# Linear attention into an eight-expert MoE: x^T stored in the order of the output rows, and output tiles that leave in one transfer

## The chip, the cores and the metric

The kernel runs on one core of a Trainium2 chip. The metric is device time in microseconds, from the start to the end of one execution. Engines are called as the profile calls them: PE is TensorE, PEld its weight loads, DVE VectorE, ACT ScalarE, POOL GpSimd, SP SyncE (which here only issues transfers). SBUF is the on-chip memory with 128 partitions, PSUM the accumulation memory of PE.

## What is computed

Inputs are q, k and v of shape (8, 8, 576, 64) (batch, head, position, channel), a gate matrix (512, 8) and two weight stacks w1 (8, 512, 1024) and w2 (8, 1024, 512). The output has 4608 rows of 512 fp32 numbers, one row for each token (8 batches of 576 positions).

```python
phi(x) = where(x > 0, x, exp(x) - 1) + 1
kv  = einsum('bhsd,bhse->bhde', phi(k), v);  z = sum(phi(k), axis=2)
num = phi(q) @ kv;  den = phi(q) . z + 1e-6
x   = (num / den), heads side by side: 4608 rows (batch, position), 512 columns
P   = exp(x @ w_gate - max)
8 times: P /= row sums; P /= column sums; P *= 4608 / 8
out = sum over e of P[:, e] * (relu(x @ w1[e]) @ w2[e])
```

## The kernel before

**Two stages that overlap.** The first is an attention front. For each batch and each group of four heads (16 units in all) `att` loads k, q and v, forms phi of k and q, and accumulates kv and z on PE (`f_kv`, L427). It transposes phi(q) on PE (L453), copies it as `qpT` (L345 or L343), multiplies it by z for the denominator and by kv for the numerator (`heads`, L482 to L486, called by `f_den` and `f_num`), and takes 1/den as exp(-ln(den)) on ACT (L497, L502). In the end `f_x` (L511 to L513) multiplies the numerator in PSUM by 1/den and writes x^T to SBUF as fp16. `xT` has the 512 channels on partitions (four blocks of 128) and all 4608 tokens along the free axis. A unit is done in two halves (c = 0, 1) of 288 tokens (CH = 288), so `f_x` runs 32 times, each over two blocks of channels, 576 elements per partition.

**The order of tokens in x^T.** k, q and v are loaded with 64 partitions for one head, partition w holding positions 9w to 9w + 8 (NJ = 9, PW = 64). Transposed, the columns stand as (j, w): all positions 9w + 0 first, then all 9w + 1, and so on. A half is a contiguous run of 288 of these columns, and x^T keeps that order, so column j * 64 + w of a batch is position 9w + j.

**The second stage** is the MoE. For expert 0 most groups of 512 tokens use plain products (L701 first layer, L996 second layer); from then on both layers use a seven-product scheme on 2 x 2 blocks, with sums and differences of blocks formed by DVE (`x_blocks` L746 to L751, `combos` L1038 and L1052, `f_S` L1083), matmuls at L816 and L1112, and DVE (L1143) or ACT with POOL (L1150, L1153) adding P times the product to the fp32 accumulators `acc`. x^T and its block differences are stored to DRAM (`xd`), and later experts load them by transfers from SP's queue (`x_load`, L793). The routing P (`logits` L529, `sinkhorn` L551 to L587) is made per token in the order of x^T; it runs on DVE and PE behind the front. Among its steps are L563, which writes its product transposed, and L586, which writes its product packed.

**Output.** Expert 7 ends the sums. `out_dma` (L967 to L974) sends a tile of 128 tokens in two transfers of 64 partitions each. The 64 tokens of a half have the same j, so their rows lie nine rows apart in the output. The transfers go by SP's queue; in the last two groups of tokens the second half goes by ACT's.

**The end.** The last group of the last expert uses plain products again (`last`, L1189 to L1222): tiles 3, 2 and 1 in whole (512 columns), tile 0 in two pieces of 256 columns, each piece with eight matmuls (L1208), a DVE step that scales and adds (L1217), and its transfers. `pl = (p_hq, p_att)[i % 2]` gives the pieces two kinds of PSUM buffers by turns.

**What sets the order.** `_Plan` is a list scheduler that runs while the kernel is built: each task has engines with a cost, what it depends on, a priority, and groups of buffers that it takes (`acq`) or uses. A buffer pool of size n lets a task take a buffer only when all users of the n-th group before are done. Numerator and `f_kv` share the pool `p_kv` of size 1. For the front, `_FRONT` (L141 to L218) writes the order of tasks out by number and engine, so that order does not depend on costs. In the later part a chain of dependencies (L1281 to L1293) fixes the order of PE's tasks, and priorities and costs decide the rest. Each engine and each queue takes its instructions in the order in which they were issued.

Of the kernel before, what the change touches and what calls it, by code (L numbers as in the profile page):

```python
# [13 lines left out]
ALU = mybir.AluOpType  # L14
# [3 lines left out]
class _Plan:  # L18
# [16 lines left out]
    def add(self, eng, fn, deps=(), prio=0.0, acq=(), use=(), lat=0.0, after=0.0, cfg=0):  # L35

        if isinstance(eng, tuple):
            eng = {eng[0]: eng[1]}
        k = len(self.t)
        t = {"eng": eng, "fn": fn, "prio": prio, "acq": tuple(acq), "lat": lat, "kids": [], "nd": 0,  # L40
             "ready": after, "done": None, "id": k, "cfg": cfg}
        self.t.append(t)
        for d in set(x for x in deps if x is not None):
            self.t[d]["kids"].append(k)
            t["nd"] += 1
        for g in list(acq) + list(use):
            g["users"].append(k)
        return k
# [173 lines left out]
def kernel(  # L222
# [10 lines left out]
    nc = tc.nc  # L233

    B, H, S, D = q.shape
# [3 lines left out]
    DM = H * D  # L239
    P = 128  # L240
    PW = 64
    NJ = S // PW
    NG = N // 512
# [7 lines left out]
    add = S_.add  # L251
# [11 lines left out]
    xT = xp.tile([P, NDT, N], FP16, tag="xT", name="xT")  # L263
# [17 lines left out]
    acc = [const.tile([P, 4, 512], FP32, tag=f"acc{g}", name=f"acc{g}") for g in range(NA)] + [None] * (NG - NA)  # L281
# [74 lines left out]
    def fadd(*a, **kw):  # L356
        t = add(*a, **kw)
        front_ids.append(t)
        return t

    CH = S // 2

    def att_bank():
        return at2[:, (len(p_att["order"]) - 1) % 2]

    def att(b, g):
# [5 lines left out]
        for nm, ten in (("k", k), ("q", q), ("v", v)):  # L372
            wide = nm == "k" or n == 0 and nm == "q"
            gr = gin[nm] = S_.grp(p_in["k" if wide else nm])
            sp = n == 0 and wide
# [44 lines left out]
        gkv, gz = S_.grp(p_kv), S_.grp(p_kvz)  # L420
# [23 lines left out]
        gq, geq = S_.grp(p_qpT), S_.grp(p_eq)  # L444
# [35 lines left out]
        grd = S_.grp(p_rden)  # L480

        def heads(dst, c, z):  # L482
            for hh in range(2):
                nc.tensor.matmul(dst[:, hh, 0:CH], lhsT=gz["tile"][:, hh, z, :],  # L484
                                 rhs=gq["tile"][:, hh, :, :].rearrange("p j w -> p (j w)")[:, CH * c:CH * c + CH],
                                 start=True, stop=True)  # L486
        tl = []
        for c in range(2):
            gd = [S_.grp(p_att), S_.grp(p_att)]

            def f_den(_, c=c):
                heads(at2, c, 1)

            def f_ln(_, c=c):
                if c == 0:
                    grd["tile"] = fp.tile([P, 2, 2, CH], FP32, tag="rden", name="rden")
                nc.scalar.activation(out=grd["tile"][:, c], in_=at2[:, :, 0:CH], func=AF.Ln, bias=eps_t)  # L497
            t1 = fadd(("pe", 0.25), f_den, deps=[tq, *tz], acq=gd, use=[gq, gz], prio=pr)
            tl.append(fadd(("act", 0.75), f_ln, deps=[t1, *tl], acq=[] if c else [grd], use=[*gd, grd], prio=pr))
# [4 lines left out]
        for c in range(2):  # L504
            gn = S_.grp(p_kv)

            def f_num(_, c=c, gn=gn):
                gn["tile"] = kvps.tile([P, 2, 512], FP32, tag="kv", name="num_ps")
                heads(gn["tile"], c, 0)

            def f_x(_, c=c, gn=gn):  # L511
                nc.vector.tensor_tensor(out=xT[:, 2 * g:2 * g + 2, S * b + CH * c:S * b + CH * c + CH],
                                        in0=gn["tile"][:, :, 0:CH], in1=grd["tile"][:, c], op=ALU.mult)  # L513
            t1 = fadd(("pe", 0.25), f_num, deps=[tq, *tz, tl[0]], acq=[gn], use=[gq, gz], prio=pr)
            xt_done[(b, 2 * g + c)] = fadd(("dve", 0.76), f_x, deps=[t1, te_], use=[gn, grd], prio=pr)

# [24 lines left out]
    def sinkhorn():  # L541
# [10 lines left out]
        for it in range(8):  # L552
# [19 lines left out]
            def f_d(_, it=it, gc=gc):  # L572
# [3 lines left out]
                else:  # L576
                    nc.vector.scalar_tensor_tensor(out=Dc, in0=Dc, scalar=EPS * float(E) / N, in1=gc["tile"],
                                                   op0=ALU.mult, op1=ALU.add)
                nc.vector.reciprocal(cc, Dc)
            a = add(("dve", 2.29 if it == 0 else 2.78), f_a, deps=last, prio=-200.0)  # L580
            c = add(("pe", 0.112), f_c, deps=[a, t_apsx], acq=[gc], prio=-200.0, lat=0.1)
            last = [add(("dve", 0.41), f_d, deps=[c], use=[gc], prio=-200.0)]

        def f_p(_):
            nc.vector.tensor_tensor(out=wt, in0=P0_sb, in1=cc[:, None, :].broadcast_to([P, NTT, E]), op=ALU.mult)
            nc.vector.tensor_tensor(out=P_sb, in0=wt, in1=Rr[:, :, None].broadcast_to([P, NTT, E]), op=ALU.mult)  # L586
        return add(("dve", 0.94), f_p, deps=last, prio=-200.0)  # L587

    nc.scalar.preload_act_table_set("natural_log_exp_and_others")
# [57 lines left out]
    def r_bank():  # L647
        return Rt[(len(p_att["order"]) - 1) % 2]
    t_apsx = add(("none", 0.0), f_apsx, deps=[*front_ids, *lg_done], prio=0.0)
    p_done = sinkhorn()  # L650
# [23 lines left out]
    fin_prev, scr_users = {}, []  # L674
# [101 lines left out]

    xst_of, xse_done, sx_users = {}, [], []

    n_load, first_x, second_x = [0], [], []

    def x_load(d, prio):
        gx = {}
# [182 lines left out]
                st["th"].setdefault(g, {0: [], 1: []})[q if dbl else m].extend(th)  # L965

    def out_dma(g, tt, deps, c0=0, cw=DM):  # L967
        for half in range(2):
            def f_o(_, half=half):
                bb, j = divmod(2 * (4 * g + tt) + half, NJ)  # L970
                dst = AP(tensor=out.tensor, offset=(S * bb + j) * DM + c0, ap=[[NJ * DM, PW], [1, cw]])
                eng = nc.scalar if g >= NG - 2 and half == 1 else nc.sync
                eng.dma_start(out=dst, in_=acc[g][64 * half:64 * half + 64, tt, c0:c0 + cw])
            add(("sp", 0.45), f_o, deps=deps, prio=900.0)  # L974

    def scale0(g, tt, deps):
        def f_s(eng, gg=4 * g + tt, g=g, tt=tt):
# [87 lines left out]
    def layer2(e, g, ui, H, th, gT, tT, uses):  # L1065
# [115 lines left out]
        if e == E - 1:  # L1181
            for tt in range(4):
                out_dma(g, tt, [fin_prev[(4 * g + tt, dh)] for dh in range(2)])
# [5 lines left out]
    def last(g, ui, H, th):  # L1189
        e = E - 1  # L1190
        gw2, tw2 = w_t[e][2:]

        def bank(gr, pl):
            if pl is p_hq:
                gr["tile"] = hqp.tile([P, 512], FP32, tag="hq", name="hq")
            else:
                gr["tile"] = r_bank().rearrange("p a b -> p (a b)")
        out_ = []
        for i, (tt, c0, cw) in enumerate(((3, 0, 512), (2, 0, 512), (1, 0, 512), (0, 0, 256), (0, 256, 256))):
            pl = (p_hq, p_att)[i % 2]  # L1200
            gr = S_.grp(pl)
            t = None
            for half in range(2):
                def f_y(_, half=half, tt=tt, c0=c0, cw=cw, gr=gr, pl=pl):
                    if half == 0:
                        bank(gr, pl)
                    for f in range(4):
                        nc.tensor.matmul(gr["tile"][:, 0:cw], lhsT=H(half)[:, f, ds(P * tt, P)],  # L1208
                                         rhs=gw2["tile"][:, 4 * half + f, c0:c0 + cw],
                                         start=(half == 0 and f == 0), stop=(half == 1 and f == 3))  # L1210
                t = add(("pe", 0.87 if cw == 512 else 0.437), f_y, deps=[*tw2, t] + th[half], acq=[gr] if half == 0 else [],
                        use=[gw2, gr], prio=ui + 0.65 + 0.01 * i)
                out_.append(t)

            def f_fin(_, tt=tt, c0=c0, cw=cw, gr=gr):
                dst = acc[g][:, tt, c0:c0 + cw]
                nc.vector.scalar_tensor_tensor(out=dst, in0=gr["tile"][:, 0:cw], scalar=P_sb[:, 4 * g + tt, e:e + 1],  # L1217
                                               in1=dst, op0=ALU.mult, op1=ALU.add)
            t = add(("dve", 0.75 if cw == 512 else 0.48), f_fin, deps=[t, p_done, fin_prev[(4 * g + tt, 0)], fin_prev[(4 * g + tt, 1)]],
                    use=[gr], prio=ui - 400.0)  # L1220
            out_dma(g, tt, [t], c0, cw)
        return out_  # L1222
# [61 lines left out]
    for n in range(-1, len(steps)):  # L1284
        for x in (order if n < len(steps) - 1 else final):
            key = (n + 1, x.lower()) if x[0] == "A" else (n, x)
            if key in pe_id:
                chain.append(pe_id[key])
    n = len(steps)
    chain += [pe_id[(n, x)] if x[0] == "y" else tail[int(x[1:])]  # L1290
              for x in "y1 y5 z0 y2 y6 z1 y3 z2 z3 y7 z4 z5 y4 z6 z7 z8 z9".split()]
    for d, k_ in zip(chain, chain[1:]):
        S_.dep(k_, d)  # L1293

# [33 lines left out]
```

## Time and profile before

| what | value |
|---|---|
| median of 3 runs | 956.34 us (956.24 to 957.54) |
| the profiled execution | 955.83 us, span 954.1 us |
| granted PE clock | 1.00 |
| PE busy | 944.5 us, 7008 matmuls |
| DVE busy | 775.0 us, 1500 instructions |
| ACT busy | 582.8 us, 1033 instructions |
| L512, the x^T write | 32 instructions, 16.9 to 121.0 us, 754 ns each |
| L484, denominator and numerator | 128 matmuls of 288 columns |
| L973, output transfers | 65 issues by SP (median 537 ns), 9 by ACT (median 552 ns) |
| last DVE step (L1217) | starts at 949.11 us, 0.48 us |

The span is the time between the first and the last recorded event of the core; the rest of an execution's time lies around it. The busy time of matmuls counts each from its issue to its modelled end, so neighbours overlap, and a PE at 99% is not a PE at its peak. A group of instructions is shown with its line, engine, operation, what it writes and reads, the shape (partitions x elements per partition), the count, the busy time and the mean of one, and then the idle time of that engine just before, with what ended it.

### The profile page before, as it was taken

To read this page: it belongs to the slowest core of one execution; us is meant where nothing else is said; L and a number is where in the kernel's file an instruction comes from. 1 tells how busy PE (TensorE), PEld (TensorE's weight loads), DVE (VectorE), ACT (ScalarE), POOL (GpSimd) and SP (SyncE) were. 2 spreads that over 40 slices of the span, in tenths; PEclk is the share of its full clock that TensorE was granted. 3 is DMA by queue.
4 is the path that set the end of the run, shared out by engine and by line. 5 is a ranking of instruction groups with operands and counts; after the bars stand their busy time and mean duration, and the time that the engine had idled before them with its cause. 6 is when DMAs were issued, how large, how long until landed. Compare 5 with 4: busy or idle time off the path is not lost.

```text
span 954.1 us, 18327 instructions
## 1 busy us (share of the span) xinstructions
PE 944.5 (99%) x7008; PEld 651.3 (68%) x7008; DVE 775.0 (81%) x1500; ACT 582.8 (61%) x1033; POOL 144.4 (15%) x209
## 2 busy tenths in 40 slices
PE   8999999999999999999999999999999999999997
PEld 4565588666677666766677666766667666776665
DVE  6899999979887888778888888878887888877775
ACT  7999766766655555555555555555555555555552
POOL 6432000011111100111111111111112111111110
PEclk9999999999999999999999999999999999999999
DMA  9998863552245222652227222542226422215544
GB/s 247 262 240 192 196 164 106 122 121 80 78 106 100 78 79 78 161 122 78 78 74 131 79 79 78 149 102 71 70 69 147 114 79 78 72 46 166 166 134 132
DMA packets 81507, 112.64 MB, mean 118 GB/s; under 512 B 7436, under 2 KB 45196, under 8 KB 81420
## 3 DMA queue, kind: packets, MB, share of 16 engines
q1 hardware_dynamic: 56844, 75.65, 26.0%
q0 software_dynamic: 23856, 34.78, 19.5%
q8 instruction: 54, 0.88, 0.4%
q10 hardware_dynamic: 720, 1.05, 0.3%
q14 instruction: 33, 0.27, 0.1%
HBM read 119.69 MB, written 17.69 MB: 144 GB/s over the span
## 4 chain that ended last, share of the span: by engine, by line
PE 97%; ACT 1%; DVE 1%; issue 0%; DVEq 0%
PE ye L1112 36%; PE hq L816 24%; PE R L816 12%; PE Zye L1112 6%; PE Zye L816 6%; PE ye L996 3%; PE hq L701 3%; PE kv_ps L427 1%; PE yw L603 1%; PE att L484 1%; PE num_ps L484 1%; PE att L453 1%; PE hq L1208 0%; PE att L529 0%; ACT rden L497 0%
## 5 line engine op out<-in xcount | busy, mean ns | idle before, releaser
L1143 DVE SCALAR_TENSOR_TENSOR acc<-ye,P_sb,acc 128x256 f32<-128x256 f32 x620 | 268.0, 478 | 127.1 <-PE ye L1112 125.2
L1112 PEld LDWEIGHTS <-S 128*128 128x128 f16 x1984 | 194.0, 98 | 46.6 <-DVE S L1083 0.2
L1112 PE MATMUL ye<-T,S 128*128 128x256 f16 x1488 | 192.8, 273 | 0.0
L1112 PEld LDWEIGHTS <-hb 128*128 128x128 f16 x1584 | 155.0, 98 | 43.0 <-issue 1.3
L1153 POOL TENSOR_TENSOR acc<-acc,st 128x256 f32<-128x256 f32 x124 | 88.3, 731 | 633.7 <-ACT st L1150 622.5
L816 PEld LDWEIGHTS <-W 128*128 128x128 f16 x1248 | 122.1, 98 | 86.0
L847 ACT ACTIVATE hb<-hq 128x512 f16<-128x512 f32 x134 | 80.0, 597 | 140.8 <-PE hq L816 137.2
L816 PE MATMUL R<-xs,W 128*128 128x512 f16 (+1 forms) x560 | 150.0, 358 | 0.0
L816 PE MATMUL hq<-xs,W 128*128 128x512 f16 (+1 forms) x560 | 150.0, 358 | 0.0
L816 PE MATMUL hq<-xs,w 128*128 128x512 f16 (+1 forms) x560 | 139.7, 358 | 0.0
L816 PEld LDWEIGHTS <-w 128*128 128x128 f16 x936 | 91.6, 98 | 59.4 <-issue 0.5
L844 ACT ACTIVATE hb<-Zye 128x512 f16<-128x512 f32 x134 | 80.1, 598 | 40.4 <-PE Zye L816 40.2
L1150 ACT ACTIVATE st<-Zye,P_sb 128x256 f32<-128x256 f32 x124 | 52.5, 471 | 76.7 <-PE Zye L1112 76.5
L850 DVE CUSTOM_DVE_ANT_0 hb<-hq,sx 128x512 f16<-128x512 f32 x126 | 86.4, 686 | 15.5 <-PE hq L816 15.3
L837 ACT COPY sx<-hq 128x512 f32<-128x512 f32 x126 | 73.5, 583 | 35.3 <-PE hq L816 35.3
L833 ACT COPY Zye<-hq 128x512 f32<-128x512 f32 x134 | 77.8, 580 | 21.1 <-PE hq L816 20.7
L850 DVE CUSTOM_DVE_ANT_0 hb<-R,sx 128x512 f16<-128x512 f32 x126 | 86.2, 684 | 4.9 <-ACT sx L837 3.8
L1083 DVE TENSOR_TENSOR S<-hb 128x1024 f16<-128x1024 f16 x124 | 84.7, 683 | 5.1 <-ACT hb L847 5.1
L816 PE MATMUL Zye<-xs,w 128*128 128x512 f16 (+1 forms) x280 | 75.0, 358 | 0.0
L841 ACT COPY sx<-R 128x512 f32<-128x512 f32 x126 | 74.4, 591 | 0.0
L1112 PE MATMUL ye<-w,hb 128*128 128x256 f16 x528 | 68.4, 273 | 0.5 <-DVE acc L1143 0.5
L1112 PE MATMUL Zye<-w,hb 128*128 128x256 f16 x528 | 68.4, 273 | 0.0
(120 smaller groups left out, 977.8 us busy)
## 6 DMA issues: line engine op xcount, KB each, us to landing
xs<-xd SPq DMA_DIRECT2D x196, 256.0 KB, 3.5
kin<-in_k_dram POOLq DMA_DIRECT2D x15, 576.0 KB, 6.9
w<-in_moe_w_dram POOLq DMA_DIRECT2D x16, 512.0 KB, 7.7
out_dram<-acc SPq DMA_DIRECT2D x63, 128.0 KB, 2.4
w<-in_moe_w_dram POOLq DMA_DIRECT2D x7, 1024.0 KB, 9.9
xs<-xd SPq DMA_DIRECT2D x49, 128.0 KB, 3.4
vv<-in_v_dram POOLq DMA_DIRECT2D x16, 288.0 KB, 7.0
hb<-in_q_dram POOLq DMA_DIRECT2D x15, 288.0 KB, 7.2
```

What stands on the lines that cost most here:

```text
L816: nc.tensor.matmul(dst_[:, p, :] if parts == 2 else dst_.rearrange("p a b -> p (a b)"), lhsT=lhs(p, c), rhs=blk[i](c), start=(first and p ...
L833: nc.scalar.copy(out=Zt[1], in_=gX["tile"])
L837: nc.scalar.copy(out=gs2["tile"], in_=gX["tile"])
L841: nc.scalar.copy(out=gs5["tile"], in_=gR["tile"])
L844: nc.scalar.activation(out=dst(0, 0), in_=Zt[1], func=AF.Relu)
L847: nc.scalar.activation(out=dst(1, 0), in_=gX["tile"], func=AF.Relu)
L850: nc.vector._custom_dve(TENSOR_ADD_SAT, out=out_, in0=ps, in1=sb, s0=3.0e38, s1=0.0)
L1083: nc.vector.tensor_tensor(out=Sx[:, i], in0=a0, in1=a1, op=op)
L1112: nc.tensor.matmul(bank(g_)[:, s, :], lhsT=lhs(s, kk), rhs=rhs(kk), start=(new and s == 0 and kk == 0), stop=(kk == 3), skip_group_check=True)
L1143: nc.vector.scalar_tensor_tensor(out=dst(), in0=bank(g_)[:, s, :], scalar=P_sb[:, gg, e:e + 1], in1=dst(), op0=ALU.mult, op1=ALU.add)
L1150: nc.scalar.mul(out=gst["tile"], in_=bank(g_)[:, s, :], mul=P_sb[:, gg, e:e + 1])
L1153: nc.gpsimd.tensor_tensor(out=dst(), in0=dst(), in1=gst["tile"], op=ALU.add)
```

## The change

Four edits.

1. The numerator and denominator matmuls of a half take positions by w instead of by j: half c reads, for all nine j, the columns w = 32c to 32c + 31 of `qpT`. The operand is nine runs of 32 elements, 64 elements apart, where it was one run of 288. The result in PSUM is packed as before, in the order (j, w).
2. `f_x` writes x^T in the order of positions. It reads numerator and 1/den packed and writes element (j, w) to column 9w + j of the half: neighbouring elements of a run of 32 land 9 elements of fp16 (18 bytes) apart. A half still fills the same 288 columns. All that reads x^T reads it as before, and tokens, P and accumulators follow the order of the output rows.
3. A tile of 128 tokens is then 128 neighbouring rows of the output, and `out_dma` sends it as one transfer of 128 partitions. In the last two groups of tokens the transfers alternate between ACT's and SP's queue.
4. In `last`, the second piece of tile 0 (256 columns) becomes two pieces of 128 columns. The costs given to the planner are written as functions of the width, and the chain of PE's tasks has two more entries.

In the changed file one line is added before `att_bank` and two in `f_x`; the lines behind them move by one or two, or stay where `out_dma` becomes shorter.

```diff
     CH = S // 2
+    CW = PW // 2
...
         def heads(dst, c, z):
             for hh in range(2):
-                nc.tensor.matmul(dst[:, hh, 0:CH], lhsT=gz["tile"][:, hh, z, :],
-                                 rhs=gq["tile"][:, hh, :, :].rearrange("p j w -> p (j w)")[:, CH * c:CH * c + CH],
-                                 start=True, stop=True)
+                nc.tensor.matmul(dst[:, hh, 0:CH].rearrange("p (j w) -> p j w", j=NJ), lhsT=gz["tile"][:, hh, z, :],
+                                 rhs=gq["tile"][:, hh, :, CW * c:CW * c + CW], start=True, stop=True)
...
             def f_x(_, c=c, gn=gn):
-                nc.vector.tensor_tensor(out=xT[:, 2 * g:2 * g + 2, S * b + CH * c:S * b + CH * c + CH],
-                                        in0=gn["tile"][:, :, 0:CH], in1=grd["tile"][:, c], op=ALU.mult)
+                dst = xT[:, 2 * g:2 * g + 2, S * b + CH * c:S * b + CH * c + CH].rearrange("p h (w j) -> p h j w", j=NJ)
+                nc.vector.tensor_tensor(out=dst, in0=gn["tile"][:, :, 0:CH].rearrange("p h (j w) -> p h j w", j=NJ),
+                                        in1=grd["tile"][:, c].rearrange("p h (j w) -> p h j w", j=NJ), op=ALU.mult)
...
     def out_dma(g, tt, deps, c0=0, cw=DM):
-        for half in range(2):
-            def f_o(_, half=half):
-                bb, j = divmod(2 * (4 * g + tt) + half, NJ)
-                dst = AP(tensor=out.tensor, offset=(S * bb + j) * DM + c0, ap=[[NJ * DM, PW], [1, cw]])
-                eng = nc.scalar if g >= NG - 2 and half == 1 else nc.sync
-                eng.dma_start(out=dst, in_=acc[g][64 * half:64 * half + 64, tt, c0:c0 + cw])
-            add(("sp", 0.45), f_o, deps=deps, prio=900.0)
+        n_out[0] += 1
+
+        def f_o(_, eng=nc.scalar if g >= NG - 2 and n_out[0] % 2 else nc.sync):
+            dst = AP(tensor=out.tensor, offset=P * (4 * g + tt) * DM + c0, ap=[[DM, P], [1, cw]])
+            eng.dma_start(out=dst, in_=acc[g][:, tt, c0:c0 + cw])
+        add(("sp", 0.45), f_o, deps=deps, prio=900.0)
...
-        for i, (tt, c0, cw) in enumerate(((3, 0, 512), (2, 0, 512), (1, 0, 512), (0, 0, 256), (0, 256, 256))):
+        for i, (tt, c0, cw) in enumerate(((3, 0, 512), (2, 0, 512), (1, 0, 512), (0, 0, 256), (0, 256, 128), (0, 384, 128))):
...
-                t = add(("pe", 0.87 if cw == 512 else 0.437), f_y, deps=[*tw2, t] + th[half], acq=[gr] if half == 0 else [],
+                t = add(("pe", 0.0017 * cw), f_y, deps=[*tw2, t] + th[half], acq=[gr] if half == 0 else [],
...
-            t = add(("dve", 0.75 if cw == 512 else 0.48), f_fin, deps=[t, p_done, fin_prev[(4 * g + tt, 0)], fin_prev[(4 * g + tt, 1)]],
+            t = add(("dve", 0.2 + 0.00108 * cw), f_fin, deps=[t, p_done, fin_prev[(4 * g + tt, 0)], fin_prev[(4 * g + tt, 1)]],
...
-              for x in "y1 y5 z0 y2 y6 z1 y3 z2 z3 y7 z4 z5 y4 z6 z7 z8 z9".split()]
+              for x in "y1 y5 z0 y2 y6 z1 y3 z2 z3 y7 z4 z5 y4 z6 z7 z8 z9 z10 z11".split()]
```

More of the change, by code (lines that the diff above doesn't have):

```diff
@@ L777 @@
     xst_of, xse_done, sx_users = {}, [], []
-    n_load, first_x, second_x = [0], [], []
+    n_out, n_load, first_x, second_x = [0], [0], [], []
     def x_load(d, prio):
```

## The prediction

> **What bounds the kernel now.** I read the page's busy table first, then its 40 slices, then the chain that ended last: PE (TensorE) is busy for 99% of the span and 97% of the chain is PE.
>
> ```profile
> PE 944.5 (99%) x7008; PEld 651.3 (68%) x7008; DVE 775.0 (81%) x1500; ACT 582.8 (61%) x1033; POOL 144.4 (15%) x209
> ...
> PE   8999999999999999999999999999999999999997
> ...
> DVE  6899999979887888778888888878887888877775
> ACT  7999766766655555555555555555555555555552
> ...
> PE 97%; ACT 1%; DVE 1%; issue 0%; DVEq 0%
> ```
>
> The reader is to see two regimes. From about slice 8 on, DVE and ACT have room and PE sets the pace alone; an output transfer there costs nothing unless PE waits for it, and the list of waits after 125 us has no PE wait on an xs load or on an output. In slices 2 to 6 (to about 120 us, the attention front) DVE stands at 8 to 9 tenths next to a full PE. The edit to the x^T write falls just there, so I then asked for busy times of DVE by stretch.
>
> ```profile
> core 0: us, DVE busy (x), PEclk, DMA share, GB/s
> 16.00:20.00 4.00, 3.44 (x6) 1.00 1.10 253
> 20.00:40.00 20.00, 17.03 (x29) 1.00 1.18 239
> 40.00:60.00 20.00, 18.27 (x30) 1.00 1.16 271
> 60.00:80.00 20.00, 18.20 (x33) 1.00 1.01 204
> 80.00:100.00 20.00, 18.79 (x37) 1.00 0.83 217
> 100.00:122.00 22.00, 19.14 (x34) 1.00 0.87 180
> 122.00:140.00 18.00, 17.49 (x38) 1.00 0.67 187
> ```
>
> The columns after the stretch are its length, DVE's busy time and the number of its instructions. Idle DVE time from 16 to 122 us is 0.56 + 2.97 + 1.73 + 1.80 + 1.21 + 2.86 = 11.1 us. The granted clock is 1.00 throughout.
>
> **Part 1: the strided x^T write (L512).** The groups by line (to 125 us) give its present cost and the idle time of DVE ahead of it; the list of waits, below it, who waits for it (total, times, longest).
>
> ```profile
> L512 DVE TENSOR_TENSOR xT<-num_ps,rden 128x576 f16<-128x576 f32 x32 | 24.1, 754 | 5.2 <-PE num_ps L484 4.5 <-ACT hb L706 0.4
> ```
>
> ```profile
> PEld L427 <- DVE xT L512: 0.5, 2, 0.2
> ```
>
> There are 32 such instructions of 754 ns for 576 elements. They now write with a step of nine 2-byte elements, 18 bytes. No row of before has a 2-byte write with such a step. The nearest pair is in the routing: L563 and L586 both multiply 288 fp32 elements by a broadcast Rr, but L563 writes transposed, with a step of 36 x 4 = 144 bytes, and L586 packed.
>
> ```profile
> L563 DVE TENSOR_TENSOR wt<-P_sb,Rr x8: 664/671/677, 127.4 to 177.2; 128x288 f32<-128x288 f32 x8
> ```
>
> ```profile
> L586 DVE TENSOR_TENSOR P_sb<-wt,Rr x1: 459/459/459, 179.8 to 179.8; 128x288 f32<-128x288 f32 x1
> ```
>
> The operands match, so the step of the output costs 671 - 459 = 212 ns, 0.736 ns an element. For 576 elements that is 424 ns: an L512 of about 1180 ns. Below, the price is bounded by zero (the instruction reads PSUM at about 1 ns an element anyway, and a write could hide behind that; nothing in it becomes less work, so no gain). Above, a second slot for every element: from L586 (459 ns, 288 elements) to L512 (754 ns, 576) a packed element takes 295/288 = 1.02 ns, so a second one costs 590 ns. I take 424, the price of the one pair that differs in nothing else, and keep 0 and 590 for the range.
>
> The Trainium skill has two rules here that differ. "SBUF — State Buffer", section "Door 1: The DMA port swizzle", says SBUF has lines of 16 bytes and that an access which goes to a new line each time pays; by it an 18-byte step pays like the 144-byte one, and the L563 row agrees that such a write pays. "VectorE: DVE Perf Modes", section "Mode 1× (REGULAR)", says that the baseline mode gives one result a cycle whatever the strides; by it L512 would keep its 754 ns and the front would not move, and the 671 ns of L563 speak against it.
>
> All 32 add 32 x 0.424 = 13.6 us to DVE between 16.9 and 121 us. How much reaches PE? num and kv_ps share one PSUM buffer (the pool of size 1), so PE's next num or kv_ps cannot start before L512 has read it. Queued behind L512 on DVE are t, tq, qpT, kvz and the relu copies, all wanted by PE or ACT. I walked one dense stretch by its timeline. L512 starts at 53.38, 54.74, 58.72 and 60.65 us, with DVE back to back from 54.06 to 64.7. The fourth ends at 61.40 and kv_ps starts at 61.45, PEld having waited 0.24 us for it. With four longer writes (+1.70) that end is about 63.1, and kv_ps and everything behind it on PE is about 1.65 us later. The next wait of DVE (0.61 us before L512 at 65.33) is for PE's num, which is as late, so it absorbs nothing. The next pair (65.33 and 66.66, +0.85) meets a wait of 0.31 before 71.37; some 0.5 is left. That is 2.15 of 2.55, 84%.
>
> From 40 to 100 us (5 + 6 + 5 = 16 instructions): 16 x 0.424 x 0.84 = 5.7 us. The other 16 (2 + 6 before 40 us, 8 after 100) are looser: the waits for PE's num or ACT's hb ahead of them (0.50, 0.34, 0.36, 0.60, 0.35, 0.50, 0.84: 3.5 us) can take up that much: 16 x 0.424 - 3.5 = 3.3 us. **Sum: +9.0 us.** The ends are 13.6 - 11.1 = 2.5 us if every idle moment of DVE could be used, and 13.6 if none. PE does not win it back later: it is busy 17.99 of the 18 us after the front, and DVE 17.49.
>
> **Part 2: the numerator and denominator matmuls (L484)** read qpT in runs of 32 elements instead of one run of 288; counts and columns are unchanged (64 + 64). A pair takes 0.25 us in the chain. Nearest row: L427 reads runs of 64 and does 18 matmuls of 192 columns in 0.85 us, no slower than its columns (two halves of 64 rows at a time). I take nothing; the upper bound, each of the 128 twice as long, is 128 x 0.123 = 15.7 us on PE. Readers of x^T (L529, L701, the block differences) see the same shapes, only other tokens in them, and P follows the same order.
>
> **Part 3: output transfers.** By the order of instructions SP issues 32 fewer and ACT 4 fewer, each about 0.54 us; the bytes stay. They lie beside PE for the whole last expert. The x loads behind them on SP's queue go out no later, with the same waits; no PE wait on such loads exists, so this gives nothing until the tail. An issue for 128 rows is no dearer than for 64: the xs loads, 128 rows, take 364 ns in the median, the outputs 537.
>
> The Trainium skill, "DMA: Bandwidth & Descriptors", section "Rules for kernel authors", says two transfers of partition halves share the same engines, so one of 128 partitions is better; that would bring nothing here before the tail, where the sum has it anyway.
>
> **Part 4: the tail.** The end of before is one 256-column piece, its DVE step, and two half transfers.
>
> ```profile
> 948.04 1.04 PE L1208 MATMUL hq<-w,hb 128*128 128x256 f16 x8
> 948.24 0.48 DVE L1217 SCALAR_TENSOR_TENSOR acc<-R,P_sb,acc 128x256 f32<-128x256 f32 x1
> 949.11 0.48 DVE L1217 SCALAR_TENSOR_TENSOR acc<-hq,P_sb,acc 128x256 f32<-128x256 f32 x1 [0.39 <-PE hq L1208]
> ```
>
> Two pieces of 128 columns: 16 matmuls at 55 ns (L453: nine of 128 columns, each with its own weights, in 0.50 us) make 0.88 us, as 8 of 256 do now. DVE's last step falls from 0.48 to about 0.34 us (512 columns take 0.75, 256 take 0.48: 1.06 ns a column), so it ends near 949.45, not 949.59. Today the later half goes out on ACT at 950.1, because ACT is still issuing the half before it; SP could take the last piece near 949.65. Landing is 2.9 us (SP) or 2.7 (ACT) for these 64 KB, and 2.9 for the xd store of 512-byte rows, so I leave it alike. Gain 0.45 us; bounds 0 and 0.8.
>
> **Sum.** The profiled execution took 955.83 us (span 954.1): 955.83 + 9.0 - 0.45 = 964.4. It lies 0.5 under the median of the three runs (956.34), so **964.9 us** is my forecast.
>
> **Rivals.**
> 1. *The write hides behind the PSUM read* and L512 stays near 754 ns. For it: L512 takes its 1.02 ns an element with an operand in PSUM, and the transposed write was measured with both operands in SBUF, so SBUF may have been the limit there. Against it: 671 against 459 with equal operands. Then only the tail is left: 956.34 - 0.45 = 955.9 us, not slower. It decides below about 0.11 us a write: 1.9 us (0.2%, about what a measurement of this kernel can tell from no change) + 0.45, over 32 x 0.66 (9.0 of 13.6). Chance 0.17.
> 2. *The price is there, but smaller or mostly covered*: DVE's 11.1 idle us take it down to +2.5, or half the price at the walked shares: 956.34 + 2.5 - 0.45 = 958.4, up to about 960.5. For it: DVE does work between that nobody needs at once (the block differences). Against it: the stretch walked above, where PE waited for L512 already. Chance 0.18.
> 3. *L484 pays for its short runs*, with PE the place: up to +15.7 on top, 980. Against it: L427. Chance 0.04.
> 4. *The forecast* (0.3 to 0.6 us a write, mostly exposed; at 590 ns 18.9 us are added, and 9.0 + 5.3 = 14.3 if all of the rest is exposed: 970): 0.61.
>
> That the transfers are not what the change says can be excluded by the order: 128 x 512 in one issue.
>
> **How the numbers follow.** Range 955.6 to 971: the no-cost end with a little of the tail's spread, and the dearest write; outside lie rival 3 and a stray tail. Within the bound or faster is rival 1 alone (0.17), of which 0.02 for a tail that gives over 1.9 us, out of only 4.5 us after the last DVE step. The likeliest case's own range is 961 to 971.
>
> **What would show it.** L512 near 1180 ns and 13 to 14 us more DVE time up to 135 us; a front some 9 us longer, with waits of PE and its weight loads on xT (now 0.5 us for kv_ps, 0.2 for num_ps) grown to several; from there to the tail, unchanged spacing; the last L1217 at about 0.34 us and some 4.2 us from its end to the end of the span. I am wrong if L512 stays at 754 ns, if it grows and PE waits no longer, or if L484's pair takes more than 0.25 us.

## The result, and the profile after

The changed kernel takes 1018.45 us (median of 5 runs, 1016.98 to 1019.26) against 956.24 before: ratio 1.0648, 95% interval 1.0633 to 1.0664. The forecast was 964.9 us in a range of 955.6 to 971. The direction was right and the size was not: 62 us were lost where 8.6 were expected. The profiled execution took 1018.12 us with a span of 1016.3.

From the page of the changed kernel: the busy row, the rows of 40 slices (of 25.4 us now) and the chain's shares.

```profile
PE 958.6 (94%) x7016; PEld 657.3 (65%) x7016; DVE 834.9 (82%) x1501; ACT 584.0 (57%) x1033; POOL 145.0 (14%) x209
...
PE   7676767899999999999999999999999999999998
...
DVE  6998998999798878887878788887888778877776
ACT  6664664467666555555555555555555555555552
...
PEclk8997998999999999999999999999999999999999
...
PE 85%; DVE 13%; issue 1%; ACT 0%; DVEq 0%
```

PE is at 6 to 7 tenths in the first seven slices, where it was at 8 or 9; from the ninth on it is at 9 as before. DVE holds 13% of the chain, where it held 1%. The page's groups by line, and the list of PE's waits to 200 us (total, times, longest), name the instruction:

```profile
L513 DVE TENSOR_TENSOR xT<-num_ps,rden 128x576 f16<-128x576 f32 x32 | 86.5, 2702 | 6.8 <-PE num_ps L485 6.2
```

```profile
PE num_ps L485 <- DVE xT L513: 24.2, 17, 2.1
PE kv_ps L428 <- DVE xT L513: 16.7, 11, 2.3
```

The x^T write (L513 in the new file) went from 754 to 2702 ns. Thirty-two times 1.948 us is 62.3 us on DVE. PE now waits for it 41 us, where before PE and its weight loads together waited 0.7 us for it. The first product of the second layer into `Zye` (L1112), just behind the front, starts at 193.0 us instead of 130.8, which is 62.2 later (after min/median/max of one product stand the first and last start; before, then changed):

```profile
L1112 PE MATMUL Zye<-w,hb x528: 270/273/273, 130.8 to 939.2; 128*128 128x256 f16 x176
L1112 PE MATMUL Zye<-w,hb x528: 270/273/273, 193.0 to 1003.0; 128*128 128x256 f16 x176
```

Another 1.6 us is lost soon behind it: the first L1112 product of `T` and `S` starts at 259.6 us instead of 195.8, which is 63.8 later.

The tail won more than expected. The last DVE step ends at 1013.27 instead of 949.59 us (63.7 later), and from there to the end of the span it is 3.0 us, where it was 4.5:

```profile
1012.92 0.35 DVE L1217 SCALAR_TENSOR_TENSOR acc<-R,P_sb,acc 128x128 f32<-128x128 f32 x1
```

The account closes: 955.83 + 63.7 - 1.5 = 1018.0, for 1018.12 measured.

### The profile page after: what moved, and what is told of

Its sections match the earlier page's. It is cut to its first block, busy times and chain, and to the rows that moved or that the text cites. A ratio compares the mean times of both kernels' runs of the same rounds, so it can differ in the third digit from the quotient of the medians.

```text
span 1016.3 us, 18299 instructions
## 1 busy us (share of the span) xinstructions
PE 958.6 (94%) x7016; PEld 657.3 (65%) x7016; DVE 834.9 (82%) x1501; ACT 584.0 (57%) x1033; POOL 145.0 (14%) x209
## 4 chain that ended last, share of the span: by engine, by line
PE 85%; DVE 13%; issue 1%; ACT 0%; DVEq 0%
PE ye L1112 34%; PE hq L817 22%; PE R L817 11%; DVE xT L513 7%; PE Zye L1112 6%; PE Zye L817 6%; PE hq L702 1%; PE ye L996 1%; PE kv_ps L428 1%; PE yw L604 1%; PE att L454 1%; DVE tq L469 1%; DVE t L407 1%; DVE t L403 1%; DVE hb L709 1%
## 5 line engine op out<-in xcount | busy, mean ns | idle before, releaser
L1112 PEld LDWEIGHTS <-S 128*128 128x128 f16 x1984 | 194.0, 98 | 46.6 <-DVE S L1083 0.2
L1112 PE MATMUL ye<-T,S 128*128 128x256 f16 x1488 | 192.8, 273 | 0.0
L1112 PEld LDWEIGHTS <-hb 128*128 128x128 f16 x1584 | 154.9, 98 | 43.0 <-issue 1.3
L513 DVE TENSOR_TENSOR xT<-num_ps,rden 128x576 f16<-128x576 f32 x32 | 86.5, 2702 | 6.8 <-PE num_ps L485 6.2
L1112 PE MATMUL ye<-w,hb 128*128 128x256 f16 x528 | 68.4, 273 | 0.5 <-DVE acc L1143 0.5
```

Of the source, the lines that this page charges most:

```text
L513: nc.vector.tensor_tensor(out=dst, in0=gn["tile"][:, :, 0:CH].rearrange("p h (j w) -> p h j w", j=NJ), in1=grd["tile"][:, c].rearrange("p ...
L1112: nc.tensor.matmul(bank(g_)[:, s, :], lhsT=lhs(s, kk), rhs=rhs(kk), start=(new and s == 0 and kk == 0), stop=(kk == 3), skip_group_check=True)
```

## The experiments

My theory after the result: the write with a step of 18 bytes is the whole loss, because of a price on narrow, scattered writes to SBUF that the routing's 4-byte write shows only in part. Rivals: the bytes of the step alone matter; the short runs of the pattern matter (in the write, or in the matmul operand); the output transfers or the split cost something. The times of before that stand beside a run are those of the same chip.

### One part undone: the write packed (e1_packed)

```diff
-                dst = xT[...].rearrange("p h (w j) -> p h j w", j=NJ)
+                dst = xT[...].rearrange("p h (j w) -> p h j w", j=NJ)
```

> The changed kernel with one thing undone: the x^T write is packed again (its order inside a half is (j, w), so the rows of the output come in another order than the reference's). The short runs of the matmul operand, the single output transfers and the split last piece stay. If the strided write is the whole loss: the write takes 754 ns, the front is as long as before, and only the tail is left: 956.2 - 1.5 = 954.7 us (the stretch from the end of the last vector step to the end of the span fell from 4.5 to 3.0 us, and that step ends 0.14 earlier: up to 1.6). If the matmuls with short runs or the other order of transfers cost as well: above 957.5.

954.67 us (954.14 to 955.41, 11 runs) against 956.29; ratio 0.9985, interval 0.9976 to 0.9994. L513 is back at 757 ns and the matmul operand with short runs costs nothing: L485 stays at 286 ns.

```profile
L513 DVE TENSOR_TENSOR xT<-num_ps,rden x32: 747/757/758, 17.3 to 120.7; 128x576 f16<-128x576 f32 x32
L485 PE MATMUL num_ps<-qpT,kvz x64: 282/286/286, 16.6 to 120.4; 128*128 128x288 f16 x64
```

So the strided write is the whole loss, and the other edits together are worth 1.6 us.

### The price of single instructions (m1_forms, m2_forms)

Both kernels hold only lines like these, on tiles that are already on chip (`st(o, s)` takes every s-th element, `n3` is the numerator's form in PSUM, `b3` 1/den's in SBUF):

```python
nc.vector.tensor_tensor(out=h16, in0=n3, in1=b3, op=ALU.mult)
nc.vector.tensor_tensor(out=h16.rearrange("p h (w j) -> p h j w", j=9), in0=n4, in1=b4, op=ALU.mult)
nc.vector.tensor_tensor(out=st(o16, 4), in0=n3, in1=b3, op=ALU.mult)
nc.vector.tensor_tensor(out=st(o32, 9), in0=n3, in1=b3, op=ALU.mult)
```

> This kernel leaves the whole computation out (its output is zeros) and only runs single instructions on data already on chip, each form twice, so that the profile shows the price of each form alone: a product of 576 elements per partition, numerator form in PSUM, with outputs of 2 or 4 bytes at several steps. In the changed kernel the strided x^T write took 2702 ns, packed 754. Theory A (narrow writes): a 2-byte write that is not joined with its neighbour costs an extra pass over its word; then 2-byte outputs with steps of 4, 8, 18 and 72 bytes all take about 2700 ns, and 4-byte outputs with steps of 36 or 72 bytes take about 1180 ns or less (the price of the routing's transposed write, 0.74 ns an element). Theory B (new line each time): what counts is the step in bytes, not the width; then 2-byte outputs at 4 and 8 bytes stay between 754 and 1180, and 4-byte outputs at 20 and 36 bytes take about 2700 too. Theory C (short runs): the nine runs of 32 in the pattern cost the time; then the packed rows of 34 in runs of 32 take about 2700 and a plain step of 18 bytes takes 754. The step on the reading side (numerator and 1/den read with a step of 128 bytes, output packed): A 754, B 1180 to 2700.

In the first kernel all forms on DVE share one line of a helper, so they cannot be told apart. The four on ACT can: 639 ns packed, 2672 with the x^T pattern, 797 with a step of 4 bytes, 1181 for 4-byte elements at 36 bytes. ACT pays what DVE pays, so this is no matter of one engine's modes. The second kernel has one line for each form.

> The computation is left out (the output is zeros); the same kind of single instructions as in m1_forms, but in a written order and each form on a line of its own, three times: 576 elements per partition each. Seen so far: x^T write with a step of 18 bytes 2702 ns, reads of 4 bytes at 128 bytes 1153 ns; on ACT a 2-byte copy with the x^T pattern 2672 ns, a 4-byte one at 36 bytes 1181, a 2-byte one at 4 bytes 797, packed 639. Theory A (narrow writes): 2-byte outputs cost about 2700 ns at any step from 4 bytes on, pairs of them (4 bytes) at most 1180. Theory B (new 16-byte line each time, whatever the width): 2-byte and 4-byte outputs cost the same at the same byte step, 754 up to 8 bytes, and 2700 from 16 bytes on. Theory D (both: past 16 bytes the step costs a second slot for 4-byte elements and four for 2-byte ones): 4-byte outputs from 16 bytes on about 1180, 2-byte ones from 16 bytes on about 2700, pairs about 1180 or less; steps below 16 bytes in between. Theory C (short runs of 32): about 2700 for the packed rows of 34 and 754 for the plain 18-byte step. The source (PSUM or SBUF) makes no difference by A, B and D.

Its answers by line, each form three times (duration min/median/max, first and last start). By line: L52 packed, L53 the x^T pattern, L54 packed runs of 32, L55 adjacent pairs every 36 bytes, L56 to L59 2-byte elements at 4, 8, 12 and 16 bytes, L60 at 18 bytes, L65 and L68 4-byte elements at 8 and 36 bytes, L73 a read of PSUM at 128 bytes, L74 a read of SBUF at 128 bytes:

```profile
L52 DVE TENSOR_TENSOR o<-num,b x3: 694/757/758, 51.2 to 136.3; 128x576 f16<-128x576 f32 x3
L53 DVE TENSOR_TENSOR o<-num,b x3: 2672/2676/2680, 51.9 to 137.0; 128x576 f16<-128x576 f32 x3
L54 DVE TENSOR_TENSOR o<-num,b x3: 757/759/759, 54.6 to 139.8; 128x576 f16<-128x576 f32 x3
L55 DVE TENSOR_TENSOR o<-num,b x3: 757/757/758, 55.4 to 140.5; 128x576 f16<-128x576 f32 x3
L56 DVE TENSOR_TENSOR o<-num,b x3: 796/797/798, 56.2 to 141.3; 128x576 f16<-128x576 f32 x3
L57 DVE TENSOR_TENSOR o<-num,b x3: 1434/1435/1435, 57.0 to 142.2; 128x576 f16<-128x576 f32 x3
L58 DVE TENSOR_TENSOR o<-num,b x3: 2068/2068/2071, 58.5 to 143.6; 128x576 f16<-128x576 f32 x3
L59 DVE TENSOR_TENSOR o<-num,b x3: 2703/2706/2708, 60.6 to 145.7; 128x576 f16<-128x576 f32 x3
L60 DVE TENSOR_TENSOR o<-num,b x3: 2672/2672/2674, 63.3 to 148.5; 128x576 f16<-128x576 f32 x3
...
L65 DVE TENSOR_TENSOR o<-num,b x3: 758/758/758, 74.7 to 159.8; 128x576 f32<-128x576 f32 x3
...
L68 DVE TENSOR_TENSOR o<-num,b x3: 1179/1180/1180, 77.9 to 163.0; 128x576 f32<-128x576 f32 x3
...
L73 DVE TENSOR_TENSOR o<-num,b x3: 757/757/757, 85.3 to 170.4; 128x576 f16<-128x576 f32 x3
L74 DVE TENSOR_TENSOR o<-num,o x3: 1110/1110/1116, 86.1 to 171.2; 128x576 f16<-128x576 f32 x3
```

The reader is to see that width and step count together. A 2-byte write grows with its step (797, 1435, 2068, 2706) and is nearly flat from 16 bytes on (2672 at 18, 2706 at 20, 2569 at 32, 2677 at 72); a 4-byte write is free at 8 bytes and nearly flat from 16 on (1170 at 16, 1239 at 72, 1175 at 144). Packed runs of 32 cost nothing, so theory C falls; a plain step of 18 bytes costs what the x^T pattern costs. A source in SBUF changes nothing (2673). Theories A and B fall too, each on a row of the other kind: A on 797 at 4 bytes, B on 1180 against 2672. Theory D is left; it describes the rows and gives no reason for them. Pairs of 2-byte elements every 36 bytes are free (757), cheaper than D's bound.

The Trainium skill, "SBUF — State Buffer", section "Door 1: The DMA port swizzle", gives lines of 16 bytes; the flat part from 16 bytes on agrees. It also says that 2-byte elements (bf16) can be up to 8 elements apart for free, and there the rows differ (1435 ns at 8 bytes, four elements) and decide.

### Order made by the matmul operand (e2_pe_order)

```diff
-                nc.tensor.matmul(dst[:, hh, 0:CH].rearrange("p (j w) -> p j w", j=NJ), lhsT=gz["tile"][:, hh, z, :],
-                                 rhs=gq["tile"][:, hh, :, CW * c:CW * c + CW], start=True, stop=True)
+                nc.tensor.matmul(dst[:, hh, 0:CH].rearrange("p (w j) -> p w j", j=NJ), lhsT=gz["tile"][:, hh, z, :],
+                                 rhs=gq["tile"][:, hh, :, CW * c:CW * c + CW].rearrange("p j w -> p w j"), start=True, stop=True)
```

(`f_x` is packed on both sides.)

> The changed kernel, but the tokens are put in order by the matmul operand: it reads element (w, j) with an inner step of 128 bytes (nine elements, then the next w), so numerator, 1/den and x^T are all packed. All other edits stay and the output is the reference's. If the step costs nothing on the reading side of the matmul: 128 matmuls keep their pace (a pair 0.25 us), and the time is that of the packed write, about 954.7 us. If each element on a new line costs a second slot: a pair takes 0.5 us, 64 pairs add 16 us, about 970 us, in a front that PE bounds. If it costs four slots as on the writing side: a pair 1.0 us, 48 us more, about 1003 us.

999.62 us (4 runs), ratio 1.0453 (1.0439 to 1.0467). In its chain from 40 to 60 us a pair takes 0.97 us (start, length, what):

```profile
43.73 0.97 PE num_ps L485 x2
44.70 0.97 PE att L485 x2
```

That is 1.68 ns for each of 2 x 288 columns, about four times the 0.25 us of a pair before. 64 pairs x 0.72 = 46 us; 999.62 - 954.67 = 45. So PE, reading 2-byte elements of SBUF 128 bytes apart, pays about as much as DVE and ACT do when they write them 16 bytes apart or more.

### Order made by reads on DVE (e3_read_step)

```diff
-                dst = xT[...].rearrange("p h (w j) -> p h j w", j=NJ)
+                dst = xT[...].rearrange("p h (w j) -> p h w j", j=NJ)
...
-                                        in1=grd["tile"][:, c].rearrange("p h (j w) -> p h j w", j=NJ), op=ALU.mult)
+                                        in1=grd["tile"][:, c].rearrange("p h (j w) -> p h w j", j=NJ), op=ALU.mult)
```

(and the same for `in0`)

> The changed kernel, but the vector engine's product writes x^T packed in the order of positions and reads numerator (PSUM) and 1/den (SBUF) with a step of 128 bytes. Output as the reference's. Theory A (narrow writes cost): reads are 4 bytes wide, the instruction stays near 754 ns, total about 954.7 us. Theory B (new line each time): 1180 to 2700 ns; at 1180 the working of the prediction gives 9 us more (about 964), full exposure 13.6 (about 968); at 2700 the total is that of the changed kernel, 1018.

964.24 us (4 runs), ratio 1.0085 (1.0071 to 1.0098). By line:

```profile
L513 DVE TENSOR_TENSOR xT<-num_ps,rden x32: 1120/1153/1174, 17.1 to 130.3; 128x576 f16<-128x576 f32 x32
```

This is, almost exactly, the price that the prediction put into its sum: 0.397 us more a time, 12.7 in all, against 0.424 and 13.6. It cost 964.24 - 954.67 = 9.6 us, 75% of what it adds. The prediction's exposure (9.0 of 13.6, 66%) was close at this dose. By the table nearly the whole price is the read of 1/den from SBUF (1110 ns); the read of the numerator from PSUM is free (757).

### Half the dose (e4_half_dose)

```diff
+                ....rearrange("p h (w j) -> p h j w" if c else "p h (j w) -> p h j w", j=NJ)
```

> The changed kernel with every second x^T write packed (the second half of a unit strided, the first packed; rows of the output in another order): 16 x 1.95 = 31.2 us added to the vector engine, half of the changed kernel's 62.3. The reads with a step added 12.7 us and cost 9.6 (76%), the full change 62.3 and cost 63.8 (102%). If the share of idle time is a fixed amount that is used up first (about 3 us): 954.7 + 28 = 983 us. If the share stays 76%: 978.4. If a slower PE clock in the gaps adds to it at this dose too: 986 or more, with a granted clock under 1.00 in the front.

985.46 us (4 runs), ratio 1.0309 (1.0293 to 1.0325): 30.8 us over e1_packed for 31.2 added, 99%. With e3_read_step (75%) and the changed kernel (63.8 for 62.3, 102%), neither a fixed share nor a fixed amount of cover fits.

The traces show where the 102% comes from. The first product into `Zye` starts at 131.1 us in e1_packed, 140.8 in e3_read_step, 161.8 here and 193.0 in the changed kernel. Up to there the three lose 9.7, 30.7 and 61.9 us, or 76%, 98% and 99% of what was added: the cover is 3 us at the small dose and about half a microsecond at the larger ones, and never negative. The changed kernel loses 1.5 us more behind the front, where the others lose nothing. PE waits there twice for a DVE that is behind:

```profile
PE hq L817 <- DVE hb L851: 0.5, 1, 0.5
PE R L571 <- DVE hb L851: 0.5, 1, 0.5
```

More work on DVE did not use up its idle time. From 16 us to the end of the front (122.4, 132.1, 153.1 and 184.3 us) DVE was idle for 10.9 us in e1_packed, 8.4 in e3_read_step, 12.0 here and 15.6 in the changed kernel. From 20 to 40 us the granted clock was 1.00 in e3_read_step, 0.94 here and 0.77 in the changed kernel; no run holds the clock apart, so what it adds stays open.

### The transfers and the tail (e5_one_transfer, e6_no_split, e7_split_only)

e5_one_transfer keeps the kernel before up to its output:

```diff
+            r0, r1 = (S * (h // NJ) + h % NJ for h in (2 * (4 * g + tt), 2 * (4 * g + tt) + 1))
+            dst = AP(tensor=out.tensor, offset=r0 * DM + c0, ap=[[(r1 - r0) * DM, 2], [NJ * DM, PW], [1, cw]])
```

> The kernel before with its x^T order (packed write, one run of 288 for the matmuls), but with the other two edits of the change: each tile of 128 tokens in one transfer (the output side steps two rows apart in the first dimension and nine rows in the second), and the last half tile in two pieces. Output as the reference's. If only the number of transfers and the split matter in the tail: 954.7 us, as with the packed write. If neighbouring rows in the output are what makes the transfer quick: 955.5 to 956.3.

1060.57 us (4 runs), ratio 1.1095 (1.108 to 1.111): far from both. The issues take 4.9 us (median) instead of 0.54, and PE waits for x loads that stand behind them on SP's queue (lines of the issue, then of PE's waits after 800 us):

```profile
L974 SPq DMA_DIRECT2D out_dram<-acc x33: 511/4937/9986, 857.7 to 1045.6; - x33
```

```profile
PE R L817 <- DMA xs<-xd: 39.1, 3, 18.2
```

The last DVE step ends at 997.9 us, 48 later than before, and from there the outputs alone take 61 us to the end of the span, where it was 4.5. So one transfer for a tile is cheap only in the plain form [128 rows]; with a first dimension of 2 on the output side it is the dearest edit of all. The Trainium skill, "DMA: Bandwidth & Descriptors", section "Rules for kernel authors", says that the slowest dimension sets how many DMA engines a transfer uses, so this one would get two; the long issues fit that, but no run here shows the engines, and it is only argued.

e6_no_split is e1_packed with the last half tile in one piece; e7_split_only is the kernel before with only the split:

```diff
-        for i, (tt, c0, cw) in enumerate(((3, 0, 512), (2, 0, 512), (1, 0, 512), (0, 0, 256), (0, 256, 128), (0, 384, 128))):
+        for i, (tt, c0, cw) in enumerate(((3, 0, 512), (2, 0, 512), (1, 0, 512), (0, 0, 256), (0, 256, 256))):
```

> As e1_packed (rows of the output in another order), but the last half tile stays one piece of 256 columns. If the split gives what the prediction gave it (0.14 us of vector time): 954.8 us, and the stretch after the last vector step stays at 3.0 us. If the split is the gain: back to 956.0 or more.

> The kernel before with only the split of the last half tile; transfers stay halves of 64 partitions. If the single transfers are the gain of the tail: 956.1 us, or slightly above 956.3, since two more transfers of about 0.55 us each stand in the queues at the end. If the split is the gain: about 954.9.

e6_no_split: 955.04 us (954.08 to 956.64, 11 runs) against 956.05; ratio 0.9989 (0.998 to 0.9998). e7_split_only: 956.30 us against 956.05; ratio 1.0002 (0.9993 to 1.0011). The single transfers alone gain 1.0 us, the split alone nothing.

The split is not without effect, though. In the profile of e7_split_only the last issue starts only at 951.4 us, 2.0 us behind the last DVE step, with two more half transfers ahead of it; the span then ends 3.0 us later, where it was 4.0 before (950.1 to 954.1). Pieces of 128 columns end with 3.0 us in e1_packed and in the changed kernel too. So the shorter stretch and the later issue cancel in e7_split_only. The profile of e6_no_split is of its slowest run, and its 4.5 us behind the last issue need not hold for the others, nine of which lie between 954.08 and 955.27; what the split adds to the single transfers (0.4 us between e6_no_split and e1_packed) is inside the spread of the runs and stays open. Output issues of e1_packed and of the kernel before, by line, show what the single transfers save:

```profile
L973 SPq DMA_DIRECT2D out_dram<-acc x33: 332/357/1793, 858.1 to 949.9; - x33
```

```profile
L973 SPq DMA_DIRECT2D out_dram<-acc x65: 466/537/1498, 857.7 to 949.8; - x65
```

An issue of 128 neighbouring rows takes 0.36 us where 64 rows took 0.54, and there are about half as many. In e1_packed the last issue starts at 949.9 us, at once behind the last DVE step (end 949.89); before, the later half waited for the half ahead of it until 950.1, half a microsecond behind a step that ended at 949.59.

### The reorder moved to reads of PSUM (e8_psum_step)

The table says where a reorder is free: in reads of PSUM. The denominator is read from PSUM by ACT's logarithm, the numerator by DVE's product; 1/den then lies in the new order and is read packed.

```diff
-                nc.scalar.activation(out=grd["tile"][:, c], in_=at2[:, :, 0:CH], func=AF.Ln, bias=eps_t)
+                nc.scalar.activation(out=grd["tile"][:, c].rearrange("p h (w j) -> p h w j", j=NJ), in_=at2[:, :, 0:CH].rearrange("p h (j w) -> p h w j", j=NJ), func=AF.Ln, bias=eps_t)
...
+                dst = xT[...].rearrange("p h (w j) -> p h w j", j=NJ)
+                nc.vector.tensor_tensor(out=dst, in0=gn["tile"][:, :, 0:CH].rearrange("p h (j w) -> p h w j", j=NJ),
+                                        in1=grd["tile"][:, c].rearrange("p h (w j) -> p h w j", j=NJ), op=ALU.mult)
```

> The changed kernel with its output in full, but the reordering is done by reads of PSUM: the logarithm on ACT reads the denominator, and the product on the vector engine reads the numerator, from PSUM with a step of 128 bytes; 1/den and x^T are written and read packed. In the table of single instructions the product with that read takes 757 ns, as packed (a read from SBUF with the step 1110). If PSUM reads are as free on ACT: L497 stays at 740 ns, L513 at 757, total 954.7 us as with the packed write, and faster than the kernel before (956.2). If ACT pays as the vector engine does for SBUF (0.6 to 0.7 ns an element): 32 x 0.4 = 12.7 us more on ACT, which is as full as the vector engine in the front: about 964 us. If four slots: above 1000.

954.80 us (954.05 to 955.65, 11 runs) against 956.30; ratio 0.9986 (0.9977 to 0.9994). By line:

```profile
L497 ACT ACTIVATE rden<-att,eps_t x32: 733/740/753, 12.8 to 117.1; 128x576 f32<-128x576 f32 x32
L513 DVE TENSOR_TENSOR xT<-num_ps,rden x32: 748/757/758, 17.6 to 121.0; 128x576 f16<-128x576 f32 x32
```

Both instructions cost what they cost packed, x^T is in the order of the output rows, and the tail's gain is kept. Against the kernel before this is a gain of 1.5 us, or 0.14%: clear of the interval, but small, and the runs of the two overlap (955.65 the slowest here, 955.55 the fastest before).

## Why the prediction was wrong, point by point

- **What bounds the kernel.** Right for the kernel before: a full front, and a PE-bound rest that hardly moves (1.5 us).
- **Part 1, the price of the write: the step that failed.** "I take 424, the price of the one pair that differs in nothing else" is the term that was mis-sized: it measured 1948 ns. The pair of rows differed from L512 in one thing that I passed over, the width of the element: L563 writes 4 bytes, L512 writes 2. (Its longer step and its operands in SBUF change little by the table: 1175 ns for 4-byte elements at 144 bytes, 2673 for 2-byte ones from SBUF.) The number was even right for its own kind: about 1180 ns was worked out, and a 4-byte write at 36 bytes takes 1180. The upper bound failed with it: "a second slot for every element" supposed one more slot, where 2-byte elements 16 bytes apart or more take about four (2706 ns). A bound drawn from an assumed mechanism was no bound.
- **Part 1, the exposure.** 66% was near the 75% that e3_read_step shows at nearly the supposed dose. With 1.948 in place of 0.424, the same working gives 16 x 1.948 x 0.84 + (16 x 1.948 - 3.5) = 53.9 us instead of 9.0, where 63.8 were lost. So 45 us of the miss are the price and 10 are the exposure. At the true dose nearly all is exposed: the idle time of DVE is no store of slack, since most of it is DVE waiting for PE, which is late as well (6.7 of 11.1 us from 16 to 122 us before, 12.3 of 15.6 from 16 to 184 us now). The dense stretch that was walked by hand (97% of the first four writes exposed) was the better guide than the loose ones.
- **Part 2, short runs of the matmul operand.** Right: 286 ns before and in e1_packed. Rival 3 needed single elements, not runs, far apart (e2_pe_order).
- **Part 3, transfers.** Right that PE does not feel them before the tail; "no dearer" was too careful, as an issue of 128 rows is shorter by a third.
- **Part 4, the tail.** 1.6 us instead of 0.45. The last DVE step took 0.35 us, as forecast (0.34); the term that was too small is the stretch behind it, taken as 4.2 us and measured as 3.0. Shorter and fewer issues give 1.0 us without the split; the split alone gives nothing; in its profile the later last issue takes back what the smaller piece wins.
- **Rivals 1 and 2.** Refuted by the 2702 ns, and the cover of rival 2 by 61.9 of 62.3 us lost in the front. For the range, the dearest case should have stood well beyond a second slot, as no row showed a 2-byte write with a step.

## What to carry to other kernels

Before a row is taken as the price of a strided access, compare the width of the element as well as the step: here, from a step of 16 bytes on, 4-byte writes cost half as much again (757 to 1180 ns) and 2-byte writes three and a half times as much (2672). If an order must change, change it where PSUM is read, or keep 2-byte elements in adjacent pairs; both were free here. And where two engines are nearly full and hand each other one buffer, count a longer instruction on that path at its full length: here 16 writes that grew by 1.95 us each were exposed to 98%, 32 that grew by 0.4 us to 76%.

## What the runs showed of the hardware

- 576 2-byte elements written to SBUF took 757 ns packed, 1435 at a step of 8 bytes and 2558 to 2708 from 16 bytes on, on DVE; on ACT packed 638 and in the x^T pattern (18 bytes) 2670. 4-byte elements took 1170 to 1239 from 16 bytes on (DVE). Adjacent pairs of 2-byte elements every 36 bytes took 757.
- A read with a step of 128 bytes was free from PSUM (DVE 757, ACT 740 ns) and cost 1110 ns from SBUF (DVE).
- A matmul whose moving operand has each 2-byte element 128 bytes from the last took 0.48 us for 288 columns instead of 0.12.
- A packed write of 4-byte elements took 951 ns, longer than with a step of 8 bytes (758). No run explains that.
